# A three-stage kernel on one core: the first pair of token blocks by plain products, the sums and differences of w_in's blocks made later

## The chip, the cores and the metric

One core of a Trainium2 chip runs the whole program. The metric is device time in microseconds (us). Five engines work side by side, each through its own instructions in order: TensorE (PE in the profile), VectorE (DVE), ScalarE (ACT), GpSimd (POOL) and SyncE (SP), which here issues every DMA.

## What is computed

Attention within chunks of 64 tokens, then a two-matrix block with a squared Relu, then a gated block. The inputs q, k and v and the output are float32, the weights float64. The reference, cut to what matters:

```python
scores = scale * np.matmul(q_c, k_c.transpose(0, 1, 2, 4, 3))   # 8 batches, 8 heads, 9 chunks of 64, head size 64
attn = np.exp(scores - np.max(scores, axis=-1, keepdims=True))
attn = attn / (np.sum(attn, axis=-1, keepdims=True) + 1e-09)
x = np.matmul(attn, v_c)                                        # brought to [4608 tokens, 512]
...
h = np.maximum(x @ w_in, 0.0)                                   # w_in 512 x 2048
x = h * h @ w_out                                               # w_out 2048 x 512
...
gate = 1.0 / (1.0 + np.exp(-(x @ w_gate)))                      # 512 x 1536
return gate * (x @ w_val) @ w_out2                              # 1536 x 512
```

The kernel turns the weights from float64 words into float32 itself.

## The kernel before

**Products.** Each float32 operand is split into a high and a low part in the type fp32r (`split`: ScalarE copies the high part, VectorE subtracts it from the source to get the low part, L437). A product of two operands of K = 256 is six matmuls: two slices of K, and for each high x high, low x high and high x low. The helper `product` (L628) issues them.

**Seven products instead of eight.** A matrix product of 2 x 2 blocks would take eight block products. The class `Unit` does it with seven: P1 to P7, by Winograd's form of Strassen's scheme. For this the weights need four operands: "a" (the blocks a11 and a12 as they are), "s" and "t" (sums and differences of blocks, made by GpSimd with four operations of 256 columns, L446) and "d" (half of b). The tokens need B11, B21, B22 and four differences T1 to T4. The results are put together by additions on VectorE out of the PSUM banks.

**The stage x @ w_in.** The 4608 tokens go in 6 pairs of blocks of 384 (`BL1`). For each pair `s`, eight units `g` cover the 2048 columns of w_in: unit g computes column tiles g and g + 8 for both blocks. The pair's attention (six tiles of 128 tokens: `attention`, L738 to L837) runs one pair ahead: pair 1's attention is worked between the products of pair 0. While pair 0 runs, the weights are also made: `weight_group` loads two tiles of w_in (`to_float32`, two raw tiles `wraw` of 512 KB each), decodes them (ScalarE L479 and L483, VectorE L486, L488 and L495, GpSimd L502), and makes the operands `wia`, `wis`, `wit` and `wid`, which are kept in SBUF for all six pairs. `finish1` squares the Relu of each result and stores it to DRAM (`gd`).

**Who sets the order.** Nothing is issued directly. Each helper adds a job (engine, cost, reads, writes) to a list, and `Plan.run` puts all jobs in order with a list scheduler: each engine takes the ready job that is due first, with modelled costs; a job's due time follows from the TensorE jobs that need it, which have a fixed order ("main" for the products, "att" for the attention's own nominal times). A job that writes a new SBUF buffer also needs room for it in an arena of 412 x 512 bytes per partition; `look` says how long before its due time it may take that room. Every engine then runs its jobs in the planned order, and waits by semaphores.

The order of the products within the units, in which a unit's last three stages fall among the next one's:

```python
for make in [*todo, None]:
    u, more = make() if make is not None else (None, None)
    for who, p in ((u, "P1"), (last, "P7"), (u, "P2"), (u, "P5"), (last, "P3"), (last, "P4"), (u, "P6")):
        if who is not None:
            who.stage(p)
```

The stages behind this one (x @ w_out in `Long` units from L939 on, the gated block) use the same plan and are not touched, but the plan is made anew for the whole program.

Of the kernel before, what the change touches and what calls it, by code (L numbers as in the profile page):

```python
# [14 lines left out]
ALU = mybir.AluOpType  # L15
# [36 lines left out]
class Plan:  # L52
    def __init__(self, room):
        self.jobs, self.room = [], room
# [64 lines left out]
    def run(self):  # L119
# [51 lines left out]

        def take(j):
            got = []
            for b in j.allocs:
                if b.psum:
                    if not banks:
                        break
                    b.at = banks.pop(0)
                    got.append(b)
                elif b.size:  # L180
                    if not place(b):
                        break
                    got.append(b)
            else:
                return True
            for b in got:
                give(b)
                b.at = None
            return False
# [28 lines left out]
        while done < len(jobs):  # L218
            moved = True
            while moved:  # L220
                moved = False
                for e in engines:
# [23 lines left out]
                    while ready[e] and tries < 600:  # L246
# [3 lines left out]
                        need = sum(b.size for b in j.allocs)  # L250
                        ok = True
                        if need:
                            if due - t + shift > (j.look or (self.LOOK if e == "SP" else self.NEAR)):
                                ok = False
                            else:
                                held = 0
                                for d, m in wants:
                                    if d >= due or d > t - shift + self.HOLD:
                                        break
                                    if not jobs[m].started:  # L260
                                        held += sum(b.size for b in jobs[m].allocs)
# [66 lines left out]
def tile_attention_relu2_glu(  # L328
# [201 lines left out]
    def weight_group(src, f, half, name, keep, look=None, raws=None, by=None, have=None, slots=None, done=None):  # L530
# [12 lines left out]
        for kind, words in (("a", BLK), ("s", BLK), ("t", BLK), ("d", HB)):  # L543
# [5 lines left out]
            ops[kind] = Buf(8 * words, top=keep, name=f"{name[:-1]}{kind}", op=True)  # L549

# [18 lines left out]
        finished("a")  # L569
        s1, s2, s3, s4 = ((sums, i) for i in range(4))  # L570
# [43 lines left out]
    def product(ps, ops, xs, p, n, first, cost_of, at_=None):  # L614
        kind, half = A_OF[p]
        op, x = ops[kind], xs[B_OF[p]]
# [20 lines left out]
        return job("PE", 6 * cost_of, go, reads if first else [*reads, ps], [ps], stream="main", at=at_)  # L637
# [249 lines left out]

    def units(todo):
# [126 lines left out]
    with tc.manual_schedule():  # L1015
# [3 lines left out]
        span = 7 * G1 * 6 * per1  # L1019
        gb = {}  # L1020
# [26 lines left out]
        def attend(s):  # L1047
            for i in range(2 * TILES):
                def nominal(what, i=i):
# [3 lines left out]
                    return (s - 1) * span + slot * SLOT  # L1053
# [5 lines left out]
        todo = []  # L1059
        state = {}  # L1060

        def unit1(s, g):
            def make():
                if s == 0:
                    w1[g] = weight_group(w1i, g, G1, f"wi{g}", True, look=120.0)
                more = None
                if g == 0:
                    if s == 0:
                        attend(0)
# [10 lines left out]
        units([unit1(s, g) for s in range(pairs1) for g in range(G1)])  # L1080
# [196 lines left out]
```

## Time and profile before

| what | value |
|---|---|
| runs of the kernel | median 1678.0 us of 3 (1673.94 to 1683.32) |
| the profiled execution | 1678.82 us, its span 1677.0 us |
| mean granted TensorE clock | 0.988 |
| TensorE busy | 1623.2 us (97%) |
| VectorE busy | 1397.7 us (83%) |
| ScalarE busy | 981.9 us (59%) |
| GpSimd busy | 836.7 us (50%) |
| DMA | 333.35 MB, 63.8% of 16 engines' span |

The span runs from the first to the last instruction of the profiled execution; its time has 1.8 us around it. Busy times are sums over the instructions. The page also gives the busy share in 40 equal slices of the span, as one digit each (tenths), and the TensorE clock that was granted, as a share of full speed.

### The profile page before, as it was taken

How to read it: one execution, taken by the hardware profiler on the slowest of the kernel's cores; microseconds unless marked ns; L12 is line 12 of the kernel's file. 1: busy time of each engine (PE TensorE's matmuls, PEld its weight loads, DVE VectorE, ACT ScalarE, POOL GpSimd, SP SyncE). 2: the span in 40 equal slices, each digit the busy share in tenths (PEclk: the TensorE clock that was granted, in tenths of full speed). 3: DMA queues.
4: the chain of work that ended last, by engine and by line, in shares of the span. 5: the costliest groups of instructions: out<-in, count | busy, mean ns of one | idle time of the engine just before them, and what ended most of it. 6: DMA issues, size and time to landing. Idle time of an engine off the chain costs nothing. (4 is left out here: it accounts for less than half of the span.)

```text
span 1677.0 us, 30764 instructions
## 1 busy us (share of the span) xinstructions
PE 1623.2 (97%) x10452; PEld 1458.9 (87%) x10452; DVE 1397.7 (83%) x2024; ACT 981.9 (59%) x1974; POOL 836.7 (50%) x644
## 2 busy tenths in 40 slices
PE   6798999999999999999999999999999999999998
PEld 5688999999899999999997889878888889778887
DVE  7998687768689999999999997664776856999996
ACT  6675565666567655655666566544555544454553
POOL 2643020212165345353566887743655755877662
PEclk9899999999999999999999999999999999999999
DMA  9925556585697555755994754586265569665562
GB/s 242 219 78 145 161 149 179 141 233 150 201 307 258 164 170 198 255 179 164 322 330 141 255 195 147 196 324 230 111 232 201 206 250 340 170 171 145 169 173 49
DMA packets 390798, 333.35 MB, mean 199 GB/s; under 512 B 234736, under 2 KB 325616, under 8 KB 390640
## 3 DMA queue, kind: packets, MB, share of 16 engines
q1 hardware_dynamic: 390640, 331.38, 63.8%
q8 instruction: 82, 1.34, 0.3%
q14 instruction: 76, 0.62, 0.1%
HBM read 209.13 MB, written 122.16 MB: 198 GB/s over the span
## 5 line engine op out<-in xcount | busy, mean ns | idle before, releaser
L502 POOL TENSOR_TENSOR wf__2708<-wf__2708,wr__2646 128x512 int32<-128x512 int32 x16 | 21.1, 1320 | 216.9 <-DVE wf__2708 L495 163.5
L502 POOL TENSOR_TENSOR wf__7364<-wf__7364,wr__6450 128x512 int32<-128x512 int32 x18 | 25.1, 1397 | 86.1 <-DVE wf__7364 L495 54.7
L446 POOL TENSOR_TENSOR raw__537<-raw__696,raw__537 128x384 f32<-128x384 f32 x24 | 28.7, 1211 | 59.8 <-DVE B__706 L437 26.5
L502 POOL TENSOR_TENSOR wf__6816<-wf__6816,wr__6450 128x512 int32<-128x512 int32 x18 | 28.1, 1561 | 48.7 <-DVE wf__6816 L495 31.2
L483 ACT ACTIVATE wr__6450<-wr__6450 128x512 int32<-128x512 uint32 x36 | 23.9, 664 | 0.0
L437 DVE TENSOR_TENSOR wx__7302<-ws__7507,wx__7302 128x512 fp32r<-128x512 f32 x18 | 18.6, 1032 | 4.2 <-ACT wx__7302 L432 4.2
L437 DVE TENSOR_TENSOR wx__7676<-ws__7507,wx__7676 128x512 fp32r<-128x512 f32 x18 | 17.7, 986 | 4.5 <-ACT wx__7676 L432 4.3
L446 POOL TENSOR_TENSOR ws__7507<-wf__6816,wf__7364 128x256 f32<-128x256 f32 x18 | 17.2, 956 | 0.4
L446 POOL TENSOR_TENSOR ws__7507<-ws__7507,wf__6816 128x256 f32<-128x256 f32 x18 | 16.1, 897 | 1.3
L502 POOL TENSOR_TENSOR w__669<-w__669,wraw__374 128x512 int32<-128x512 int32 x1 | 1.4, 1378 | 30.4 <-ACT B__729 L432 30.4
L437 DVE TENSOR_TENSOR wx__7419<-wf__7364,wx__7419 128x256 fp32r<-128x256 f32 x18 | 16.4, 909 | 0.0
L488 DVE TENSOR_SCALAR wf__7364<-wf__7364 128x512 int32<-128x512 int32 x18 | 15.6, 867 | 0.6
L479 ACT ACTIVATE wf__6816<-wr__6450 128x512 f32<-128x512 f32 x18 | 12.0, 664 | 6.4 <-POOL ws__7507 L446 3.3
L446 POOL TENSOR_TENSOR raw__537<-raw__537 128x384 f32<-128x384 f32 x12 | 15.1, 1275 | 0.0
L486 DVE TENSOR_SCALAR wf__7364<-wf__7364 128x512 f32<-128x512 f32 x18 | 10.6, 590 | 5.3 <-ACT wf__7364 L479 5.3
L495 DVE SCALAR_TENSOR_TENSOR wf__7364<-wr__6450,wf__7364 128x512 int32<-128x512 int32 x18 | 14.7, 818 | 0.1
L479 ACT ACTIVATE wf__2708<-wr__2646 128x512 f32<-128x512 f32 x16 | 10.8, 672 | 6.6 <-DMA wf<-wf__2708 5.2
L446 POOL TENSOR_TENSOR raw__696<-raw__696 128x384 f32<-128x384 f32 x12 | 14.6, 1235 | 0.0
L495 DVE SCALAR_TENSOR_TENSOR wf__6816<-wr__6450,wf__6816 128x512 int32<-128x512 int32 x18 | 13.9, 774 | 0.2
L417 ACT ACTIVATE c__1728<-c__1728 128x384 f32<-128x384 f32 x20 | 10.4, 520 | 6.3 <-DVE c__1728 L446 6.2
L486 DVE TENSOR_SCALAR wf__6816<-wf__6816 128x512 f32<-128x512 f32 x18 | 9.0, 502 | 6.0 <-ACT wf__6816 L479 6.0
L837 ACT ACTIVATE raw__537<-bank 128x256 f32<-128x256 f32 x36 | 12.1, 381 | 2.0 <-DVE T__973 L437 1.3
(5624 smaller groups left out, 6528.8 us busy)
## 6 DMA issues: line engine op xcount, KB each, us to landing
ad<-wx__7302 SPq DMA_DIRECT2D x27, 512.0 KB, 4.8
ad<-wx__7676 SPq DMA_DIRECT2D x27, 512.0 KB, 4.5
wr__2646<-in_moe_w_out_dram SPq DMA_DIRECT2D x16, 512.0 KB, 4.8
wr__6450<-in_moe_w_gate_dram SPq DMA_DIRECT2D x12, 512.0 KB, 5.4
wr__6450<-in_moe_w_val_dram SPq DMA_DIRECT2D x12, 512.0 KB, 4.7
wr__6450<-in_moe_w_out_dram SPq DMA_DIRECT2D x12, 512.0 KB, 3.9
ad<-wx__7419 SPq DMA_DIRECT2D x18, 256.0 KB, 4.4
wf<-wf__2708 SPq DMA_DIRECT2D x16, 256.0 KB, 5.2
```

The source lines that it names most:

```text
L417: lambda: nc.scalar.activation(out=o(), in_=i(), func=func, **kw), ib, ob, soon=soon,
L437: lambda: nc.vector.tensor_tensor(out=lo(), in0=at(src, n, F32, off), in1=hi().bitcast(F32), op=ALU.subtract),
L446: eng, cost(eng, n), lambda: e.tensor_tensor(out=o(), in0=a(), in1=b(), op=op),
L479: nc.scalar.activation(out=at(w), in_=t[:, :, 1].bitcast(F32), func=ACTF.Abs)
L483: nc.scalar.activation(out=low, in_=low.bitcast(U32), func=ACTF.Copy, scale=2.0**-29)
L486: nc.vector.tensor_scalar_max(at(w), at(w), TINY)
L488: nc.vector.tensor_scalar(out=wi, in0=wi, scalar1=5, scalar2=2, op0=ALU.logical_shift_left, op1=ALU.logical_shift_right,)
L495: nc.vector.scalar_tensor_tensor(out=wi, in0=words()[:, :, 1], scalar=-0x40000000, in1=wi, op0=ALU.bitwise_and, op1=ALU.bitwise_or,)
L502: nc.gpsimd.tensor_tensor(out=wi, in0=wi, in1=words()[:, :, 0], op=ALU.add)
L837: nc.scalar.activation(out=o[:, :, a:a + CH], in_=i, func=ACTF.Copy)
```

## The change

For pair 0 the units g = 0 to 7 are no longer `Unit`s but plain ones: `plain_unit` makes the four results of a 2 x 2 block product by eight products, each result two products into one bank. It needs the weight operands "a" (first tile of w_in, both halves) and a new "l" (`wil`, the second tile, both halves; a buffer that is free again after pair 0), and the token operands B11, B21, B12 and B22; B12 uses the slots of T1. `finish0` takes a result from its bank: Relu on ScalarE, then a square, on VectorE for two of the four results (bank times Relu), on ScalarE for the other two. The units' own order is no longer interleaved in pair 0.

In `weight_group`, "s", "t" and "d" get a longer `look` (60 instead of 30) and come behind "l" in the list; their first use is in pair 1, which sets their due times. The buffers for s and t of all eight groups are given their places at the start of the plan (`plan.first`). The attention of pair 1 is listed after the weights of unit 1, with its nominal times stretched by 8/7.

```diff
 class Plan:
     def __init__(self, room):
-        self.jobs, self.room = [], room
+        self.jobs, self.room, self.first = [], room, []
...
+        for b in self.first:
+            place(b)
...
             ops[kind] = Buf(8 * words, top=keep, name=f"{name[:-1]}{kind}", op=True)
+            if keep and not have and kind in "st":
+                plan.first.append(ops[kind])
...
         finished("a")
+        if late:
+            ops["l"] = Buf(8 * BLK, name="wil", op=True)
+            split(ops["l"], b, BLK, look=look)
+            look = late
...
+    def plain_unit(ops, xs, n, per, finish):
+        u = Unit(ops, xs, n, per, finish, "")
+        for row, col in ((0, 0), (1, 0), (0, 1), (1, 1)):
+            ps = psum("C")
+            for half in range(2):
+                multiply(ps, ops["al"[row]], half, xs[f"B{half + 1}{col + 1}"], n, half == 0, per)
+            finish(u, row, col, ps)
...
+        span0 = 8 * G1 * 6 * per1
...
-                    return (s - 1) * span + slot * SLOT
+                    if s == 1:
+                        return slot * SLOT * 8 / 7
+                    return span0 + (s - 2) * span + slot * SLOT
...
+        def finish0(g):
+            def finish(u, row, col, ps):
+                n, f = BL1, g + row * G1
+                t = sbuf(n, "e")
+                copy(u.words(t), [t], u.words(ps), [ps], n, func=ACTF.Relu)
+                if row == col:
+                    binary("DVE", u.words(t), u.words(ps), u.words(t), ALU.mult, n, [t], [t, ps])
+                else:
+                    copy(u.words(t), [t], u.words(t), [t], n, func=ACTF.Square, soon=4.0)
...
+        attend(0)
+        first_xs = {}
+        for (r, c), x in blocks1(raw1).items():
+            name = f"B{r + 1}{c + 1}"
+            first_xs[name] = slots1["T1" if name == "B12" else name]
+            for op, (src, off) in zip(first_xs[name], x):
+                split(op, src, BL1, off=off)
+        for g in range(G1):
+            w1[g] = weight_group(w1i, g, G1, f"wi{g}", True, look=30.0, late=60.0)
+            if g == 1:
+                attend(1)
+            plain_unit(w1[g], first_xs, BL1, per1, finish0(g))
...
-                if s == 0:
-                    w1[g] = weight_group(w1i, g, G1, f"wi{g}", True, look=120.0)
...
-        units([unit1(s, g) for s in range(pairs1) for g in range(G1)])
+        units([unit1(s, g) for s in range(1, pairs1) for g in range(G1)])
```

`multiply` is `product` with the operands given to it. The plan places the same kinds of jobs in another order. Three places follow, in rows of each engine's order: line of the kernel (a line of the changed kernel is some 5 to 14 higher than its like before), operation, written and read tiles. The numbers in a tile's name are its place in memory.

TensorE, from the first product of pair 0 on, before (B and T are token operands, wia, wis and wit weight operands; a row is three matmuls, half a product):

```order
L628 MATMUL bank_78<-B_3072_29696__706,wia_186368__800 128x384 x3
L628 MATMUL bank_78<-B_3072_21504__729,wia_186368__800 128x384 x3
L628 MATMUL bank_74<-B_3072_18432__750,wia_186368__800 128x384 x3
L628 MATMUL bank_74<-B_3072_26624__761,wia_186368__800 128x384 x3
L628 MATMUL bank_75<-T_3072_195584__791,wis_182272__832 128x384 x3
L628 MATMUL bank_75<-T_3072_192512__793,wis_182272__832 128x384 x3
L628 MATMUL bank_78<-T_3072_175104__871,wis_182272__832 128x384 x3
L628 MATMUL bank_78<-T_3072_172032__877,wis_182272__832 128x384 x3
L628 MATMUL bank_73<-B_3072_29696__706,wia_165888__890 128x384 x3
L628 MATMUL bank_73<-B_3072_21504__729,wia_165888__890 128x384 x3
L628 MATMUL bank_78<-T_3072_162816__918,wit_178176__836 128x384 x3
L628 MATMUL bank_78<-T_3072_159744__921,wit_178176__836 128x384 x3
```

and in the change (768 is a transpose of k or q, 785 the scores of an attention tile):

```order
L641 MATMUL bank_74<-B_3072_44032__762,wia_129024__734 128x384 x3
L641 MATMUL bank_74<-B_3072_40960__767,wia_129024__734 128x384 x3
L785 MATMUL bank_75<-kT_22528__779,qT_38912__786 64x64 x16
L641 MATMUL bank_74<-B_3072_125952__769,wia_129024__734 128x384 x3
L641 MATMUL bank_74<-B_3072_122880__777,wia_129024__734 128x384 x3
L641 MATMUL bank_73<-B_3072_44032__762,wil_18432__751 128x384 x3
L641 MATMUL bank_73<-B_3072_40960__767,wil_18432__751 128x384 x3
L641 MATMUL bank_73<-B_3072_125952__769,wil_18432__751 128x384 x3
L641 MATMUL bank_73<-B_3072_122880__777,wil_18432__751 128x384 x3
L768 MATMUL bank_77<-ident,k_51200__747 128x128 x4
L641 MATMUL bank_76<-T_3072_48128__818,wia_129024__734 128x384 x3
L641 MATMUL bank_76<-T_3072_113664__827,wia_129024__734 128x384 x3
```

Before, the first unit needs wis and T1 after two products; now it needs wia, wil and B operands alone, with the attention's groups among them.

VectorE, before, in the first unit of pair 0 (790, 791 and 794 belong to the softmax, 486, 488 and 495 to a weight's decode, 437 is the low part of a split, 446 an addition out of a bank):

```order
L437 TENSOR_TENSOR wia_186368__800<-w_38912__763,wia_186368__800 128x512
L790 TENSOR_REDUCE mx_2048__852<-bank_72 128x8
L437 TENSOR_TENSOR wis_182272__832<-sums_34816__752,wis_182272__832 128x512
L791 TENSOR_TENSOR a_108544__875<-bank_72,mx_2048__852 128x512
L437 TENSOR_TENSOR T_3072_175104__871<-raw_6144_204800__537,T_3072_175104__871 128x384
L437 TENSOR_TENSOR T_3072_172032__877<-raw_6144_204800__537,T_3072_172032__877 128x384
L486 TENSOR_SCALAR w_55296__798<-w_55296__798 128x512
L488 TENSOR_SCALAR w_55296__798<-w_55296__798 128x512
L437 TENSOR_TENSOR wia_165888__890<-w_100352__783,wia_165888__890 128x512
L794 TENSOR_REDUCE mx_2048__852<-a_108544__875 128x8
L437 TENSOR_TENSOR wit_178176__836<-sums_34816__752,wit_178176__836 128x512
L446 TENSOR_TENSOR e_110592__885<-e_110592__885,bank_74 128x384
```

and in the change, around the first split of an s operand (807 to 812 belong to the softmax, 491 to 500 to a decode, 442 is a split, 451 the finishing multiply):

```order
L442 TENSOR_TENSOR wia_83968__1454<-w_28672__1144,wia_83968__1454 128x512
L807 TENSOR_REDUCE mx_24064__1299<-a_19968__1479 128x8
L810 TENSOR_SCALAR mx_24064__1299<-mx_24064__1299 128x8
L811 RECIPROCAL mx_24064__1299<-mx_24064__1299 128x8
L812 TENSOR_TENSOR a_19968__1479<-a_19968__1479,mx_24064__1299 128x512
L442 TENSOR_TENSOR wil_96256__1477<-w_24576__741,wil_96256__1477 128x512
L491 TENSOR_SCALAR w_26624__799<-w_26624__799 128x512
L493 TENSOR_SCALAR w_26624__799<-w_26624__799 128x512
L500 SCALAR_TENSOR_TENSOR w_26624__799<-wraw_55296__444,w_26624__799 128x512
L451 TENSOR_TENSOR e_0__1553<-bank_75,e_0__1553 128x384
L442 TENSOR_TENSOR wis_206848__1107<-sums_88064__996,wis_206848__1107 128x512
L442 TENSOR_TENSOR wia_92160__1569<-w_22016__1288,wia_92160__1569 128x512
```

Before, wis and wit of a unit stand within ten rows of its wia; now wis of unit 0 (wis_206848) stands behind wil of unit 5 (wil_96256), in the second half of pair 0.

SP, before, where the loads of w_in are issued (wraw are the raw tiles of w_in, k, q and v the attention's inputs):

```order
L410 DMA wraw_51200__406<-in_moe_w_in_dram 128x4x256
L410 DMA k_512__408<-in_k_dram 128x8x64
L410 DMA q_55296__415<-in_q_dram 128x8x64
L410 DMA wraw_59392__419<-in_moe_w_in_dram 128x4x256
L410 DMA wraw_63488__429<-in_moe_w_in_dram 128x4x256
L410 DMA wraw_67584__431<-in_moe_w_in_dram 128x4x256
L410 DMA wraw_71680__452<-in_moe_w_in_dram 128x4x256
L410 DMA wraw_75776__455<-in_moe_w_in_dram 128x4x256
L410 DMA wraw_79872__464<-in_moe_w_in_dram 128x4x256
L410 DMA wraw_6144__466<-in_moe_w_in_dram 128x4x256
L410 DMA wraw_83968__475<-in_moe_w_in_dram 128x4x256
L410 DMA wraw_88064__493<-in_moe_w_in_dram 128x4x256
```

and in the change, at the loads for units 4 to 6 (gd are stores of pair 0's results):

```order
L415 DMA wraw_63488__860<-in_moe_w_in_dram 128x4x256
L415 DMA v_69120__872<-in_v_dram 128x8x64
L415 DMA gd_88<-e_67584__870 128x384
L415 DMA gd_80<-e_4608__846 128x384
L415 DMA gd_80<-e_73216__913 128x384
L415 DMA wraw_79872__934<-in_moe_w_in_dram 128x4x256
L415 DMA k_76800__944<-in_k_dram 128x8x64
L415 DMA q_19968__949<-in_q_dram 128x8x64
L415 DMA wraw_6144__625<-in_moe_w_in_dram 128x4x256
L415 DMA gd_88<-e_18432__946 128x384
L415 DMA v_85504__985<-in_v_dram 128x8x64
L415 DMA gd_81<-e_83968__983 128x384
```

Before, all sixteen loads go out before the first store; now the last six stand among the loads of the next attention and the stores of pair 0's first results.

## Rows read from the trace of the kernel before

**Rows 1.** The page, the span in 40 equal slices, busy tenths of TensorE:

```profile
PE   6798999999999999999999999999999999999998
```

**Rows 2.** Stretches: us from:to, length, busy us (instructions) by engine, granted clock, DMA:

```profile
29.87:135.30 105.43, 80.42 (x783) 71.68 (x784) 103.30 (x155) 73.85 (x155) 62.85 (x56) 0.86 0.64 165
43.19:155.03 111.84, 94.31 (x816) 86.17 (x815) 104.72 (x164) 73.97 (x157) 60.89 (x54) 0.90 0.59 147
155.03:215.00 59.97, 58.32 (x605) 54.03 (x604) 43.47 (x84) 35.19 (x77) 2.67 (x3) 1.00 0.57 154
160.00:1677.00 1517.00, 1497.49 (x9121) 1347.17 (x9119) 1257.09 (x1803) 874.54 (x1751) 763.23 (x574) 1.00 0.63 202
```

The engines stand in the order PE, PEld (weight loads), DVE, ACT, POOL.

**Rows 3.** TensorE's waits from 0 to 160 us: total us, times, longest:

```profile
PE bank L628 <- DVE e__1147 L446: 3.0, 1, 3.0
PE bank L628 <- DVE wia__800 L437: 3.0, 1, 3.0
...
PE bank L628 <- DVE T__918 L437: 2.4, 1, 2.4
```

**Rows 4.** TensorE in order of time: start, us, line, tiles, shape, count:

```profile
43.19 0.69 PE L628 MATMUL bank<-B__706,wia__800 128*128 128x384 f32 x1
...
47.66 1.16 PE L628 MATMUL bank<-B__729,wia__800 128*128 128x384 f32 x3
...
99.71 0.69 PE L822 MATMUL bank<-aT__1212,v__838 64*64 64x64 f32 x32
100.34 0.79 PE L628 MATMUL bank<-T__871,wis__1267 128*128 128x384 f32 x3
100.97 0.68 PE L628 MATMUL bank<-T__877,wis__1267 128*128 128x384 f32 x3
101.49 0.68 PE L628 MATMUL bank<-B__706,wia__1369 128*128 128x384 f32 x3
...
102.63 1.15 PE L772 MATMUL bank<-kT__1373,qT__1377 64*64 64x64 f32 x32
103.70 0.79 PE L628 MATMUL bank<-T__918,wit__1337 128*128 128x384 f32 x3
...
105.90 0.60 PE L806 MATMUL bank<-ident,a__1396 128*128 128x128 f32 x4
106.33 0.60 PE L755 MATMUL bank<-ident,k__935 128*128 128x128 f32 x4
...
154.51 0.69 PE L628 MATMUL bank<-T__973,wid__1812 128*128 128x384 f32 x3
...
156.88 0.44 PE L628 MATMUL bank<-T__871,wis__832 128*128 128x384 f32 x1 [0.46 <-DVE T__871 L437]
...
158.17 0.45 PE L628 MATMUL bank<-T__877,wis__832 128*128 128x384 f32 x1 [0.50 <-DVE T__877 L437]
```

**Rows 5.** VectorE in order of time, within one unit of pair 0:

```profile
105.73 1.78 DVE L437 TENSOR_TENSOR wis__1402<-sums__1349,wis__1402 128x512 fp32r<-128x512 f32 x1
107.44 0.68 DVE L790 TENSOR_REDUCE mx__1371<-bank 128x8 f32<-128x512 f32 x1
108.04 0.54 DVE L446 TENSOR_TENSOR b__1398<-b__1398,bank 128x384 f32<-128x384 f32 x1
108.50 0.59 DVE L437 TENSOR_TENSOR wid__1387<-w__847,wid__1387 128x256 fp32r<-128x256 f32 x1
...
110.08 0.41 DVE L486 TENSOR_SCALAR w__1470<-w__1470 128x512 f32<-128x512 f32 x1
110.52 0.43 DVE L488 TENSOR_SCALAR w__1470<-w__1470 128x512 int32<-128x512 int32 x1
110.86 0.68 DVE L437 TENSOR_TENSOR wia__1517<-w__1244,wia__1517 128x512 fp32r<-128x512 f32 x1
```

**Rows 6.** A load of w_in (KB, us from issue to landing); SP's waits, 0 to 160 us:

```profile
wraw__499<-in_moe_w_in_dram SPq DMA_DIRECT2D x1, 512.0 KB, 9.7
...
SPq L410 <- ACT raw__537 L837: 8.2, 1, 8.2
```

More of the change, by code (lines that the diff above doesn't have):

```diff
@@ L174, in take @@
             for b in j.allocs:
+                if b.at is not None:
+                    continue
                 if b.psum:
@@ L249, in run @@
                         tries += 1
-                        need = sum(b.size for b in j.allocs)
+                        need = sum(b.size for b in j.allocs if b.at is None)
                         ok = True
@@ L260, in run @@
                                     if not jobs[m].started:
-                                        held += sum(b.size for b in jobs[m].allocs)
+                                        held += sum(b.size for b in jobs[m].allocs if b.at is None)
                                 if due - t + shift > self.FAR:
@@ L528, in float32_in_dram, with weight_group @@
         return load
-    def weight_group(src, f, half, name, keep, look=None, raws=None, by=None, have=None, slots=None, done=None):
+    def weight_group(src, f, half, name, keep, look=None, raws=None, by=None, have=None, slots=None, done=None, late=None):
         by = by or columns
@@ L615, in product, with multiply @@
         kind, half = A_OF[p]
-        op, x = ops[kind], xs[B_OF[p]]
+        multiply(ps, ops[kind], half, xs[B_OF[p]], n, first, cost_of)
+    def multiply(ps, op, half, x, n, first, cost_of):
         size = op.size // 8
@@ L635, in go @@
                     )
-        return job("PE", 6 * cost_of, go, reads if first else [*reads, ps], [ps], stream="main", at=at_)
+        return job("PE", 6 * cost_of, go, reads if first else [*reads, ps], [ps], stream="main")
     def token_ops(blocks, n, slots=None):
@@ L1057, in blocks1 @@
             return {(r, c): [(raws[c], (2 * r + kk) * BL1) for kk in range(2)] for r in range(2) for c in range(2)}
-        todo = []
+        def finish0(g):
[7 more added lines that the diff above has]
+                    copy(u.words(t), [t], u.words(t), [t], n, func=ACTF.Square, soon=4.0)
+                a = col * BL1
+                d = gb[f, col] = Buf(name="g")
+                dma(lambda: gd[f][:, a:a + n], lambda: at(t), [t], [d], size=P * n * 4, soon=6.0)
+            return finish
+        attend(0)
[10 more added lines that the diff above has]
+            plain_unit(w1[g], first_xs, BL1, per1, finish0(g))
         state = {}
@@ L1063, in make @@
             def make():
-                if s == 0:
-                    w1[g] = weight_group(w1i, g, G1, f"wi{g}", True, look=120.0)
                 more = None
                 if g == 0:
-                    if s == 0:
-                        attend(0)
                     state["xs"], rest = token_ops(blocks1(raw1), BL1, slots1)
```

## The prediction

> **What bounds the kernel now.** I read the page first for the whole span, then the stretches of the first 320 us, then the waits of TensorE there, then single instructions. The page shows TensorE busy to 9 tenths or more in nearly every one of its 40 slices of 42 us, except in the first two (6 and 7), the fourth (8) and the last (8) [rows 1]. So there are two regimes: a start in which TensorE is short of operands, and some 1500 us in which it is the bound. In the stretches [rows 2] TensorE idles 1517.0 - 1497.5 = 19.5 us after 160 us, little for so long a stretch; from 155 to 215 us it idles 1.65 us in 60. The loss lies ahead of that.
>
> VectorE is why. From 29.87 us (first decode of w_in) to 135.30 us (last weight operand of pair 0) it is busy 103.3 of 105.4 us [rows 2], and TensorE's waits in the start are mostly for VectorE: for e (a bank that an addition still reads), wia (a weight operand) and T (a token operand) [rows 3].
>
> How much does TensorE lose? Pair 0's products start at 43.19 us, and the last half of its last one starts at 154.51 us [rows 4]; until 155.03 us that is 111.84 us. A product is two rows of three matmuls at 0.52 us (100.97 to 101.49), so 1.04 us; the attention in between has groups of 0.43 (four transposes), 0.63 (mixing with v) and 1.07 us (scores) [rows 4]. In that stretch stand 59 products (56 of pair 0, 3 of pair 1), 13 + 6 transposed groups, 6 scores, 6 mixes: 61.4 + 8.2 + 6.4 + 3.8 = 79.8 us. So 32.0 us are lost, in waits and in time at the lower clock: the mean granted clock there is 0.90, and at 47.66 us three matmuls show 1.16 us, at 100.97 us 0.68 [rows 2, 4].
>
> **The change, TensorE.** In pair 0 a unit goes from 7 to 8 products: 8 units x 1.04 us = 8.3 us more, all on the path, for good. The rest of TensorE's program has the same products. To compare, take "pair 0 is done". Before, by 155.03 us TensorE had also done 3 products of pair 1, and three transposed groups and one score group that the new order holds until later: 3.1 + 1.3 + 1.1 = 5.5 us. So the equal point before is 149.5 us. After, pair 0 has 64 products, 8 + 6 transposed groups, 6 scores and 6 mixes behind its first product: 66.6 + 6.0 + 6.4 + 3.8 = 82.8 us. The start stays near 43.2 us: the four raw tiles, and k and q, are still loaded one after another, and the order puts two more transposed groups ahead. The gain is 149.5 - 43.2 - 82.8 - L = 23.5 - L, where L is what TensorE will still lose.
>
> **The change, VectorE.** Alone, from start to next start [rows 5]: 0.60 us for 512 wide, 0.46 for 384, 0.44 and 0.34 for the two decode steps (0.40 in the mean); 0.35 for 256 wide, 0.22 for the small ones, from the same pattern. Before, 29.87 to 135.30 us holds 62 of 512, 44 of 384, 32 decode steps, 12 small, 6 of 256: 37.2 + 20.2 + 12.8 + 2.6 + 2.1 = 74.9 us. It took 105.4, so 30.5 us are stretching. A row shows it: wis takes 1.78 us while GpSimd works, an equal wia 0.68 [rows 5]. GpSimd was busy 62.85 us in 56 instructions, 1.12 us each [rows 2]; so each busy microsecond of GpSimd costs VectorE 30.5 / 62.85 = 0.49 us.
>
> After, from the first decode to the last row of pair 0, the order has 63 of 512 (the splits of l added; most of s and t still there, since wis and wit of units 0 to 3 are made before pair 0 ends), 23 of 384 (8 token splits instead of 14; two finishing multiplies a unit instead of five additions and squares), 32 decode steps, 12 small, 3 of 256, one transpose of 0.7: 37.8 + 10.6 + 12.8 + 2.6 + 1.1 + 0.7 = 65.6 us. GpSimd has 16 decodes and 24 sums ahead of that point, and none of the ten token differences: 40 x 1.12 = 44.8 us, which stretch VectorE by 22 us. So VectorE could be through at 29.9 + 65.6 + 22 = 117.5 us, where TensorE by its own sum is done at 43.2 + 82.8 = 126 us. **The bound moves from VectorE to TensorE**, but narrowly. By the same sums wia of unit 2 is there at about 53, unit 4 at 83, unit 6 at 99 us and wil of unit 7 at about 115; TensorE, at 10.35 us a unit and 3 us late from its start, wants them at 67, 88, 108 and 121. The margin is 5 to 14 us, and VectorE spends some of it: six times, it must wait in order for a score product, with the weight splits queued behind that wait, and a finishing multiply now waits in its queue for a product and for ScalarE's Relu. I take 1 to 6 us of margin as left.
>
> **L.** At the lower clock three matmuls took 1.16 instead of 0.68 us [rows 4], so about half of such a time is lost; for some 6 us of it at the start, 3 us. Further waits lie between 2.3 us (the rate of 155 to 215 us, 1.65 in 60 [rows 2], over 83 us) and 14 us (half of the 32.0, from the same stretch while VectorE was the bound). Nearest is the first, as the operands are early by the sum, but the margin is thin: 5 us. L = 8.
>
> **What goes to pair 1.** VectorE still has 9 splits of s and t and 5 of d behind the last row of pair 0 (9 x 0.60 + 5 x 0.35 = 7.2 us), and GpSimd 8 sums (9.0 us, 4.4 of stretch). VectorE is busy 43.5 of 60 us in that stage [rows 2], so it has 16 us spare per 60 us: covered, unless it all stands before the first T operands. Those must wait anyway for the last product that reads their slots; the same hand-over before shows waits of 0.46 and 0.50 us for T, at 156 and 158 us [rows 4]. I add 1.5 us for it, between 0 and all 11.6.
>
> **SP's queue.** Before, all 16 loads of w_in went out in a row; the longest took 9.7 us to land [rows 6]. Now the loads for units 5 to 7 stand between stores of pair 0's results, and a store waits for its unit. For about three units, 31 us, each load runs ahead of its product; landing and preparing it need 9.7 us and about 5 us of decode and split. Cost: nothing, as that lead covers it.
>
> Sum: 23.5 - 8 - 1.5 = 14.0 us gained, of the profiled execution's 1678.8 us, which lies 0.8 us above the median of the runs. From the median: **1664.0 us**. Where the tables of the later stages come out differently by the new plan, I allow 3 us either way, about a sixth of the 19.5 us idle there.
>
> **A rule that speaks against it.** VectorE's operations that read PSUM kept 0.54 us (108.04) right between stretched ones [rows 5], so it is the ones with SBUF operands that GpSimd slows. The Trainium skill (SBUF — State Buffer, "Who interferes with whom") says that the two hold a shared port as an exclusive lock, by which the later one blocks fully. The trace agrees on which operations are hit; by the lock taken at its worst, a whole microsecond lost per busy one, the 22 us of stretch would be 44.8.
>
> **The rivals.**
>
> *VectorE stays the bound.* If its remaining mix suffers a full microsecond per busy one of GpSimd instead of 0.49, it ends at 29.9 + 65.6 + 44.8 = 140.3 us, wil of unit 7 some 2 us earlier, and 6 products (6.2 us) follow: 144.5 against 149.5. With the hand-over 3.5 us stay gained, and gaps at the lower clock take most of that: 1677. For it: the share of two-operand splits in VectorE's work rises. Against: 0.49 was measured on much the same mix. Chance 0.08.
>
> *The deferred work bunches at pair 1.* If the 11.6 us all fall before the first T operands, the gain is 23.5 - 8 - 11.6 = 4: 1674. For it: five d and nine s and t splits stand among the token splits there in the order. Against: TensorE needs them one unit at a time. Chance 0.10. Waits in pair 0 near their upper end give the same (23.5 - 17 - 1.5 = 5, 1673): 0.03.
>
> *Slower: the loads turn into a ring.* A load behind a store, the store behind a product, the product behind an earlier load. SP has waited 8.2 us for a single buffer [rows 6]. The lead of 31 us covers 15 us of landing and preparing and two such waits; from a third in a row on, each of units 5 to 7 comes 8 us late, 24 us, and after each gap TensorE runs at the lower clock for a while, some 4 us lost in all: L = 8 + 28, and 23.5 - 36 - 1.5 = -14: 1692. For it: two slots of raw tiles are loaded again in the middle of pair 0, one of them twice. Against: a lead of three units. Chance 0.06.
>
> *The change does not defer.* The order shows wis of unit 0 behind wil of unit 5, so this is out; only part of the deferral is small, as s and t of four units are still made in pair 0. That is in the sum.
>
> *More than forecast.* No waits beyond the first clock ramp and no hand-over: 23.5 - 3 = 20.5, 1657.5, or less with luck later. Chance 0.07.
>
> **How the numbers follow.** Forecast (1657.5 to 1669.6) 0.66, more 0.07, the no-change rivals 0.08 + 0.10 + 0.03, slower 0.06. A difference of 0.5%, 8.4 us, is about what a measurement here can tell from none: faster means under 1669.6. Faster 0.66 + 0.07 = 0.73; same 0.21; slower 0.06. The range goes from 1655 (1657.5 less most of the 3 us) to 1678: above it lie the ring and part of the first rival, below it little.
>
> **What would show it.** Right: first product of pair 0 at 42 to 45 us; VectorE no longer filled from 60 to 120 us; GpSimd without token differences until pair 0 is over; the last half product of pair 0 at 128 to 138 us instead of 154.5; TensorE's waits for wia and wil few and under 1 us; after that the same spacing as before. Wrong: wil splits ending just as their products start, or T waits of several microseconds at pair 1; a gap on TensorE with an SP wait for a store behind it; or a gain in pair 0 that is lost again after 215 us.

## The result and the profile after

The changed kernel takes 1662.68 us, the median of 4 runs (1661.88 to 1663.56), beside 1678.37 us of 4 runs of the kernel before (1673.94 to 1683.32): ratio 0.9906, 95% interval 0.9878 to 0.9934. The forecast was 1664.0 with a range of 1655 to 1678 and 0.73 for faster by over 0.5%. The total came out as forecast, but not by the forecast's terms: the first pair of token blocks (pair 0) gained half as much again as it was to gain, and a third of that was given back behind it.

The page of the kernel after, busy tenths in 40 slices and the granted clock, beside [rows 1]:

```profile
PE   7999999999999999999999999999999999999998
DVE  7998677767789999999999797754777757999995
POOL 1552103030454443543577677733675646867672
PEclk8999999999999999999999999999999999999999
```

The second slice (42 to 83 us) went from 7 to 9 and the fourth from 8 to 9: the start has lost its holes. TensorE is busy 1621.5 us of the span of 1661.8 us (98%), where it was 1623.2 of 1677.0, although pair 0 has 8 products more: less of the work was done at the lower clock (the granted clock in pair 0 is 0.98 below, 0.90 in [rows 2]).

Stretches of the kernel after; the columns are those of [rows 2]. The first is pair 0 on TensorE, the second goes from the first decode of w_in to VectorE's last row of pair 0, the third is the rest:

```profile
39.50:126.36 86.86, 86.86 (x827) 82.92 (x826) 81.03 (x127) 70.38 (x146) 45.94 (x43) 0.98 0.70 191
29.17:121.78 92.61, 88.55 (x882) 83.35 (x883) 86.14 (x136) 76.70 (x161) 47.32 (x44) 0.94 0.74 194
155.00:1661.80 1506.80, 1479.76 (x8915) 1333.77 (x8913) 1240.75 (x1778) 864.82 (x1732) 764.61 (x578) 0.99 0.64 202
```

In pair 0 TensorE is busy 86.86 of 86.86 us; before it was 94.31 of 111.84. VectorE, filled before to 103.30 of 105.43 us, is busy 86.14 of 92.61; of the 6.5 us that it is idle, 1.6 are waits for score products and about 3 are waits for ScalarE. Behind 155 us it is the other way round: TensorE idles 1506.80 - 1479.76 = 27.0 us, where it idled 19.5 [rows 2].

TensorE in order of time (columns as in [rows 4]): the first product, the last weights of pair 0, its last half product, and the hand-over to pair 1:

```profile
39.50 1.31 PE L641 MATMUL bank<-B__762,wia__734 128*128 128x384 f32 x3
...
120.12 0.68 PE L641 MATMUL bank<-B__762,wil__1817 128*128 128x384 f32 x3
...
125.84 0.68 PE L641 MATMUL bank<-B__842,wil__1817 128*128 128x384 f32 x3
126.36 0.68 PE L641 MATMUL bank<-B__762,wia__734 128*128 128x384 f32 x3
...
134.10 0.45 PE L641 MATMUL bank<-T__2020,wis__1107 128*128 128x384 f32 x1 [0.63 <-DVE T__2020 L442]
...
135.39 0.45 PE L641 MATMUL bank<-T__2022,wis__1107 128*128 128x384 f32 x1 [0.49 <-DVE T__2022 L442]
```

Pair 0 ends at 126.36 us with none of pair 1's products done; the equal point before was 149.5 us. So 23.1 us are gained there. The spans differ by 15.2 us (1677.0 - 1661.8), so 7.9 us were given back behind pair 0. The hand-over is little of that: its two T waits above take 1.1 us, but the same two waits took 0.96 us before [rows 4]. About 7.7 us were lost later, which fits the idle time (27.0 against 19.5). Where, the stretches show. Of the kernel before:

```profile
300.00:480.00 180.00, 175.28 (x1643) 165.77 (x1643) 138.12 (x251) 113.62 (x250) 44.22 (x38) 0.98 0.68 192
480.00:800.00 320.00, 318.85 (x1834) 317.23 (x1833) 304.61 (x483) 202.21 (x424) 143.44 (x124) 1.00 0.63 207
```

and of the kernel after:

```profile
300.00:480.00 180.00, 175.12 (x1582) 166.01 (x1573) 135.38 (x245) 116.30 (x257) 49.14 (x44) 0.99 0.73 211
480.00:800.00 320.00, 314.85 (x1793) 311.19 (x1792) 309.89 (x483) 197.42 (x408) 149.49 (x122) 0.99 0.64 211
```

The idle time is alike up to 480 us, and 1.15 against 5.15 us from 480 to 800 us, where the stage with w_out begins; the rest is spread over the stretches behind. The edit does not touch that stage.

VectorE in order of time in the kernel after, up to its last row of pair 0:

```profile
101.37 0.69 DVE L803 TENSOR_REDUCE mx__1299<-bank 128x8 f32<-128x512 f32 x1 [1.00 <-PE bank L785]
...
116.90 1.23 DVE L442 TENSOR_TENSOR wit__1516<-sums__1259,wit__1516 128x512 fp32r<-128x512 f32 x1
118.05 1.22 DVE L442 TENSOR_TENSOR wil__1817<-w__1701,wil__1817 128x512 fp32r<-128x512 f32 x1
...
121.23 0.55 DVE L451 TENSOR_TENSOR e__1857<-bank,e__1857 128x384 f32<-128x384 f32 x1
```

The last wil is there at 118.05 + 1.22 = 119.27 us, 0.85 us before its first product at 120.12. The bound has moved, with little to spare.

### The profile page after: what moved, and what is told of

Read it like the earlier page. It is cut to its first block, busy times and chain, and to the rows that moved or that the text cites. A ratio compares the mean times of both kernels' runs of the same rounds, so it can differ in the third digit from the quotient of the medians.

```text
span 1661.8 us, 30842 instructions
## 1 busy us (share of the span) xinstructions
PE 1621.5 (98%) x10500; PEld 1463.8 (88%) x10500; DVE 1375.4 (83%) x2002; ACT 979.9 (59%) x1968; POOL 822.3 (49%) x636
## 5 line engine op out<-in xcount | busy, mean ns | idle before, releaser
L451 POOL TENSOR_TENSOR raw__514<-raw__674,raw__514 128x384 f32<-128x384 f32 x20 | 23.5, 1195 | 69.2 <-DVE B__762 L442 48.8
L451 POOL TENSOR_TENSOR ws__7370<-ws__7370,wf__6751 128x256 f32<-128x256 f32 x18 | 15.7, 870 | 1.3
L493 DVE TENSOR_SCALAR wf__7084<-wf__7084 128x512 int32<-128x512 int32 x18 | 14.2, 790 | 0.6
L484 ACT ACTIVATE wf__6751<-wr__6460 128x512 f32<-128x512 f32 x18 | 12.0, 665 | 4.7 <-POOL ws__7370 L451 4.7
L500 DVE SCALAR_TENSOR_TENSOR wf__7084<-wr__6460,wf__7084 128x512 int32<-128x512 int32 x18 | 14.4, 801 | 0.2
L442 DVE TENSOR_TENSOR B__762<-raw__514,B__762 128x384 fp32r<-128x384 f32 x6 | 3.4, 566 | 13.0 <-ACT B__762 L437 13.0
L484 ACT ACTIVATE wf__7084<-wr__6460 128x512 f32<-128x512 f32 x18 | 11.9, 659 | 2.8 <-DMA wr__6460<-in_moe_w_gate_dram 2.8
L484 ACT ACTIVATE wf__3381<-wr__3279 128x512 f32<-128x512 f32 x16 | 10.6, 665 | 4.3 <-DMA wf<-wf__3381 4.2
L451 DVE TENSOR_TENSOR b__12368<-b__12368,bank 128x512 f32<-128x512 f32 x5 | 3.4, 687 | 11.3 <-PE bank L641 11.3
L493 DVE TENSOR_SCALAR wf__6751<-wf__6751 128x512 int32<-128x512 int32 x18 | 12.3, 682 | 0.6
```

The costliest lines, as they stand in the source:

```text
L442: lambda: nc.vector.tensor_tensor(out=lo(), in0=at(src, n, F32, off), in1=hi().bitcast(F32), op=ALU.subtract),
L451: eng, cost(eng, n), lambda: e.tensor_tensor(out=o(), in0=a(), in1=b(), op=op),
L484: nc.scalar.activation(out=at(w), in_=t[:, :, 1].bitcast(F32), func=ACTF.Abs)
L493: nc.vector.tensor_scalar(out=wi, in0=wi, scalar1=5, scalar2=2, op0=ALU.logical_shift_left, op1=ALU.logical_shift_right,)
L500: nc.vector.scalar_tensor_tensor(out=wi, in0=words()[:, :, 1], scalar=-0x40000000, in1=wi, op0=ALU.bitwise_and, op1=ALU.bitwise_or,)
```

## The experiments

**The theory** after this result: in the start VectorE, slowed by GpSimd, was the bound; the change takes the sums and additions off it until TensorE is the bound, and that is worth 23 us. **A first rival**: the start gains because products come earlier in the order, and VectorE's load matters little. **For what was given back** there are two more: the later loss belongs to the change (late s, t and d), or it is the plan, since the scheduler writes the order of everything behind pair 0 anew.

**1. The plain products without the deferral.** Sums and splits of s, t and d are due at once, in the kernel after:

```diff
+        soon = 1.0 if late else None
...
-        split(ops["s"], sums, BLK, look=look)
+        split(ops["s"], sums, BLK, look=look, soon=soon)
```

and so for the sums, t and d.

> The changed kernel, with the s, t and d operands of each group of w_in due at once again, as the a and l operands are; pair 0 stays with plain products. Theory (VectorE sets the pace only when its queue is full; the deferral takes 9 splits of s and t, 5 of d and 8 sums out of pair 0, 11.6 us of VectorE): pair 0's last half product, at 125.8 us in the changed kernel, comes 3 to 9 us later, and the time is 1665 to 1672. Rival 1 (the plain products give the whole gain, the deferral none): 125 to 127 us and 1661 to 1665. Rival 2 (the deferral gives the whole gain): 145 us or later, 1676 or more.

Measured: 1666.87 us (1662.37 to 1669.43, 5 runs), ratio to the kernel before 0.9928 (0.9906 to 0.9951). Pair 0 in this run, on TensorE and by stretch:

```profile
134.44 0.68 PE L642 MATMUL bank<-B__837,wil__1911 128*128 128x384 f32 x3
```

```profile
39.78:134.96 95.18, 90.35 (x839) 85.04 (x837) 91.84 (x139) 75.52 (x157) 49.54 (x44) 0.97 0.71 187
```

The last half product comes 8.6 us later than in the kernel after (134.44 against 125.84), with 4.8 us of idle time in the stretch where there was none; VectorE is busy 91.84 of 95.18 us again. The largest waits are for a (2.4 and 1.2 us), the softmax whose steps stand in VectorE's queue between the splits. By its last half product this run has also done 12 transposes more of the attention than the kernel after by its own (108 against 96, three groups of 0.43 us). So the deferral does part of the work, about 7 of the 23 us of pair 0. The whole kernel, however, is only 4.2 us slower than after, within the 1665 to 1672 expected: it makes up some 3 us behind pair 0, with 23.2 us of idle time behind 155 us instead of 27.0.

**2. The kernel before without its sums.** s and t are not made, the products of pair 0 and later read a in their place:

```diff
+        if keep and not have:
+            ops["s"] = ops["t"] = ops["a"]
+            split(ops["d"], b, HB, off=HB, look=look)
+            return ops
```

> The kernel before, seven products, but s and t of w_in are not made: the products that want them read the a operand instead (the four sums of each group and the two splits behind them are left out). Theory (in the kernel before, VectorE's and GpSimd's work on these operands is what holds pair 0 up): VectorE loses 16 x 0.60 us and the stretch by 32 sums, about 24 us; the products of pair 0 start at 39 to 44 us, the equal point of 149.5 us comes at 117 to 125 us, and the time is 1648 to 1658. Rival (the loads of w_in, or the token differences, hold it up anyway): the equal point after 140 us, and 1668 or more.

Measured: 1657.86 us (one run). The last half product of pair 0 there, which is row 154.51 of [rows 4]:

```profile
133.82 0.68 PE L632 MATMUL bank<-T__928,wid__1927 128*128 128x384 f32 x3
```

It stands 20.7 us earlier than before, with TensorE's products unchanged, and the time is 19.7 us less than the 1677.55 us of the kernel before on that chip. VectorE's and GpSimd's work on s and t, not the order of the products, set the length of pair 0. The first rival falls. The run takes away the work and the products' wait for its results together, so it does not part these two. The expectation held for the time (1648 to 1658) and was too hopeful for pair 0: its equal point, reckoned as before, comes at about 128 us and not at 117 to 125, though its first product comes at 36.01 us, ahead of the 39 to 44 expected.

**3. Two more VectorE operations a unit, in the kernel after.** They are 512 wide and their result is not used:

```diff
+            for _ in range(2):
+                x = sbuf(BLK, "extra")
+                binary("DVE", lambda x=x: at(x), lambda: at(a), lambda: at(b), ALU.subtract, BLK, [x], [a, b], soon=2.0)
```

> The changed kernel with two more VectorE operations of 128x512 with two SBUF inputs in each of the eight groups of pair 0 (16 x 0.60 us and their stretch, 10 to 14 us; their results are used by nobody). Theory (TensorE is the bound in pair 0 now, and VectorE has s, t and d to put off further): pair 0's last half product at 126 to 129 us, against 125.8, and 1660 to 1668. Rival (VectorE is still the bound): 135 us or later, and 1671 or more.

Measured: 1673.81 us (one run). Pair 0's last half product, and a wait behind it:

```profile
128.82 0.68 PE L644 MATMUL bank<-B__844,wil__751 128*128 128x384 f32 x3
...
136.76 1.15 PE L788 MATMUL bank<-kT__2007,qT__1857 64*64 64x64 f32 x32 [2.46 <-ACT kT__2007 L422]
```

Pair 0 ends 3.0 us later, as expected: 16 operations, at least 9.6 us by the 0.60 us of one, are absorbed to two thirds. Room for them came from putting off more: by the end of pair 0 only 3 of the 16 splits of s and t are done and none of d, where the kernel after has 9 and 3. The total was expected at 1660 to 1668 and missed that by 6 us: 8 us are lost behind pair 0 (2.46 at once, at the hand-over, where ScalarE's copy of kT stands behind four others in its queue, and 3 us more of idle time behind 155 us than after). Whether the work put off costs this, or the new plan, is not shown.

**4. Without the fixed places for s and t.** In the kernel after:

```diff
-        for b in self.first:
-            place(b)
```

> The changed kernel without the places given to the s and t buffers at the start of the plan; they take their room when they are written. Theory (the fixed places serve the room in memory and cost pair 0 nothing): pair 0's last half product at 125 to 128 us, and 1658 to 1668, as the later stages are planned anew. Rival (64 KB more room in pair 0 brings the loads of w_in earlier and with them pair 0's end): 123 us or earlier. Rival (the room for s and t then comes late): the hand-over to pair 1 waits 5 us or more.

Measured: 1772.38 us (one run). The page, and one of TensorE's waits:

```profile
PE   7999700699999999999999999999999999999998
```

```profile
PE bank L638 <- ACT wit__3097 L434: 105.1, 1, 105.1
```

The last half product of pair 0 starts at 125.94 us, as after. But between 160 and 330 us TensorE stands still for 105.1 us in one piece, for t of the last unit. ScalarE's copy for this t stands in its queue behind twelve decodes of w_out, each of which waits 7.2 to 8.7 us for the store of the one before. The expected 1658 to 1668 failed; nearest is the rival by which the room comes late, but it priced 5 us or more, at the hand-over. The change's least visible line is what makes the deferral safe. That the plan puts t behind those decodes for want of room in SBUF is argued from what the line does; the trace shows the wait and the order.

**5. The same kernels in other plans.** In both kernels the attention of all pairs behind pair 1 (the expectations name pairs 2 and 3, the edit reaches pairs 2 to 5) is due somewhat later or earlier, and nothing else is changed. In the kernel after (shift 0.7; the others -0.7, 0.3 and 1.5):

```diff
-                    return span0 + (s - 2) * span + slot * SLOT
+                    return span0 + (s - 2) * span + slot * SLOT + 0.7
```

In the kernel before the shift is added to (s - 1) * span + slot * SLOT, for s over 1.

> The kernel after, with the due times of the attention of pairs 2 and 3 shifted by 0.7 us, and nothing else: the same work, the planner writes the order of everything behind pair 0 anew. Theory (the 7 to 8 us that went missing between the gain of pair 0, 23.1 us, and the gain of the whole, 15.2 us, are the luck of one plan): pair 0 ends within 1.5 us of 125.8, TensorE's idle time behind 155 us is not 27 but anywhere from 18 to 33 us, and the time moves by as much, 1653 to 1669. Rival (the loss belongs to the change: later s, t and d, fewer free slots, weights that come late): idle time stays at 25 to 29 us and the time within 2 us of 1662.7.

> As the run before, with a shift of 1.5 us. Theory: 1653 to 1669, idle behind 155 us 18 to 33 us, and different from the other shift by 3 us or more. Rival: 1661 to 1665 and 25 to 29 us of idle time, as after.

> The kernel before, with the same shift of 0.7 us for pairs 2 and 3. Theory: the 19.5 us of idle time behind 160 us are one plan's as well; 1671 to 1686, idle 14 to 28 us. If the plan before had been the lucky one, both shifts of it give 1680 to 1686 and both of after 1655 to 1662. Rival: within 2 us of 1677.6.

> The kernel before, with a shift of 1.5 us. Theory: 1671 to 1686, idle behind 160 us 14 to 28 us, and different from the other shift by 3 us or more. Rival: within 2 us of 1677.6.

> The kernel after, the attention of pairs 2 and 3 due 0.7 us earlier instead of later. The shifts to later cost 26 and 30 us behind pair 0 (12 us of it one wait for w_out's first operand). Theory A (luck of the plan: each plan is a draw, and the one of after was a good one): 1662 to 1692, nothing gained on average against 1662.7. Theory B (it was the direction: later attention is worse, earlier is not): within 4 us of 1662.7. Theory C (the change makes the later stages frailer than before): after's loss by this shift is more than 10 us above that of before by the same shift. In all: pair 0 ends at 125 to 127 us.

> The kernel after, shift of 0.3 us to later. A: 1662 to 1692, and not between the times of the shifts 0 and 0.7 in any order; B: 1663 to 1689, between them; C: as for the run before. Pair 0 ends at 125 to 127 us.

> The kernel before, the attention of pairs 2 and 3 due 0.7 us earlier. A: 1675 to 1692; B: 1674 to 1681; C: less loss than the kernel after has by this shift, by more than 10 us.

> The kernel before, shift of 0.3 us to later. A: 1675 to 1692; B: between 1677.6 and 1686.4; C: less loss than the kernel after has by this shift, by more than 10 us.

Measured, 4 runs each (9 of the kernel before with 0.3), medians in us, beside 1676.8 and 1677.1 of the unshifted kernel before on the same chips; "last" is the start of the last half product of pair 0, "rest" the span less that, "idle" TensorE's idle time behind 160 us (before) and 155 us (after):

| shift | before: time | last | rest | idle | after: time | last | rest | idle | difference of the times |
|---|---|---|---|---|---|---|---|---|---|
| -0.7 | 1689.27 | 155.12 | 1532.4 | 28.6 | 1659.72 | 125.46 | 1531.8 | 25.5 | -29.6 |
| 0 | 1678.37 | 154.51 | 1522.5 | 19.5 | 1662.68 | 125.84 | 1536.0 | 27.0 | -15.7 |
| 0.3 | 1684.03 | 155.09 | 1527.1 | 26.9 | 1667.95 | 126.38 | 1541.5 | 31.6 | -16.1 |
| 0.7 | 1686.36 | 154.63 | 1529.7 | 30.8 | 1689.01 | 126.38 | 1560.7 | 47.2 | +2.7 |
| 1.5 | 1687.75 | 151.08 | 1534.4 | 29.0 | 1692.31 | 126.14 | 1565.2 | 45.9 | +4.6 |

Three things follow.

The gain of pair 0 is firm: in five plans the last half product of the changed kernel starts between 125.46 and 126.38 us, that of the kernel before between 151.08 and 155.12.

The rest is not. It moves by 12 us over the plans of the kernel before and by 33 us over those of the kernel after, by shifts of 0.3 to 1.5 us. So 7.7 us lost behind pair 0 need no cause in the edit: the plan of the kernel before, with 19.5 us idle, is the best of its five. That all of it is such luck is not shown, and the pairs lean against it. In every plan 59 products are done when "last" is, before, and 64 after, so that the kernel before is ahead by 3 products of pair 1 and some attention, 5.5 us of work (5.1 with 0.7 and 3.5 with 1.5, where it has done less attention). The rest is longer after by -0.6, 13.5, 14.4, 31.0 and 30.8 us; less that work, one pair gains 6 us behind pair 0 and four lose 8 to 27. Five pairs do not part a loss by the change from the luck of the plans.

The expectations erred too: the kernel after with 0.7 and 1.5 is 20 us and more outside 1653 to 1669; the kernel before is 0.4 and 1.8 us above 1686, with 30.8 and 29.0 us idle where 14 to 28 were expected, and the two differ by 1.4 us and not by 3; with -0.7 the kernel after is below theory A's 1662 to 1692. The shift does not act like a draw on the kernel after, whose time rises with it in all five rows, as theory B said; on the kernel before it does not, since -0.7 costs 11 us there. Theory C holds for the two large shifts (26 and 30 us against 8 and 9) and fails for 0.3 (5.3 against 5.7) and for -0.7, where the kernel after loses nothing.

Where the plan with 0.7 loses, its trace shows. TensorE there:

```profile
525.54 1.20 PE L961 MATMUL bank<-x__6358,woa__6078 128*128 128x384 f32 x6
539.45 0.69 PE L961 MATMUL bank<-x__6482,woa__6101 128*128 128x384 f32 x1 [12.70 <-ACT woa__6101 L437]
540.67 1.97 PE L961 MATMUL bank<-x__6482,woa__6101 128*128 128x384 f32 x5 [0.53 <-DVE woa__6101 L442]
```

the stretch:

```profile
520.00:540.00 20.00, 7.30 (x40) 6.71 (x39) 19.53 (x26) 3.84 (x9) 13.56 (x12) 0.72 0.30 101
```

and VectorE in it:

```profile
526.93 1.21 DVE L442 TENSOR_TENSOR wod__6456<-w__5597,wod__6456 128x256 fp32r<-128x256 f32 x1
528.07 1.34 DVE L442 TENSOR_TENSOR x__6498<-g__6103,x__6498 128x384 fp32r<-128x384 f32 x1
529.33 1.07 DVE L451 TENSOR_TENSOR g__6160<-g__6383,g__6160 128x384 f32<-128x384 f32 x1
...
537.65 0.41 DVE L442 TENSOR_TENSOR wod__6473<-w__5711,wod__6473 128x256 fp32r<-128x256 f32 x1
...
540.19 0.42 DVE L442 TENSOR_TENSOR woa__6101<-w__5583,woa__6101 128x256 fp32r<-128x256 f32 x1
```

ScalarE in the same stretch:

```profile
532.30 0.52 ACT L437 ACTIVATE x__6507<-g__6115 128x384 fp32r<-128x384 f32 x1 [7.27 <-DVE wod__6465 L442]
538.57 0.52 ACT L437 ACTIVATE x__6522<-g__6130 128x384 fp32r<-128x384 f32 x1 [5.75 <-DVE wod__6488 L442]
539.00 0.40 ACT L437 ACTIVATE woa__6101<-w__5583 128x256 fp32r<-128x256 f32 x1
```

It is much like the start of pair 0, at the start of w_out: VectorE is busy 19.53 of 20 us, token differences and wod splits stand in its queue ahead of the one woa split that TensorE needs, GpSimd works beside it for 13.56 us, and a 256-wide split that takes 0.41 us takes 1.21. The long wait itself is for ScalarE's half of that split: it stands behind two token copies that wait 7.27 and 5.75 us for VectorE's wod splits. The wait of 12.7 us is about half of the 25 us that this plan loses on the plan of the kernel after; with the shift of 1.5 the same place costs 11.9 us; in the eight other plans of the two kernels no wait of TensorE from 500 to 570 us is over 3.8 us. Why a shift of attention brings those splits into that order was not traced further.

The plan with -0.7 of the kernel after is the lowest measured, 1659.72 us (1658.1 to 1661.4), ratio 0.9892 (0.9870 to 0.9914). That is 3 us below the kernel after, but the two intervals overlap.

## Why the prediction was right, and which of its terms were not

| term | predicted | measured |
|---|---|---|
| first product of pair 0 | 43.2 us | 39.50 us |
| TensorE's work in pair 0, and low clock | 82.8 us and 3 us | 86.86 us, so 4.1 over the sum, at the lower clock and in spacing |
| waits in pair 0 | 5 us | none |
| pair 0 done, gain on 149.5 us | 134 us, 15.5 us | 126.36 us, 23.1 us |
| hand-over to pair 1 | 1.5 us | 1.1 us, 0.2 more than before |
| later stages | 0, within 3 us | 7.7 us lost |
| sum | 14.0 us | 15.2 us of the spans |

**The mechanism** stood as put: the bound of pair 0 was VectorE and is TensorE now. Experiment 2 shows the first half by itself, the stretch of 86.86 us without idle time the second.

**VectorE's sum** was nearly exact. It was forecast to be busy 65.6 + 22 = 87.6 us up to the last row of pair 0, and was for 86.14 us, in 136 instructions where 134 were counted. GpSimd was busy 47.32 us there (44.8 forecast); (86.14 - 65.6) / 47.32 = 0.43 us of stretch for each of its busy microseconds, against 0.49 (which counts 2.1 us of VectorE's idle time as stretch; (103.3 - 74.9) / 62.85 is 0.45). The end at 121.78 instead of 117.5 us is waiting in order, 6.5 us in all, which the prediction named (score products, ScalarE's Relu) but did not add.

The prediction's worst case, a whole microsecond for each busy one of GpSimd, would be 65.6 + 47.3 = 112.9 us in a stretch of 92.61, and did not come. Single rows are blocked in full all the same. In the kernel before:

```profile
44.59 1.66 POOL L502 TENSOR_TENSOR w__774<-w__774,wraw__386 128x512 int32<-128x512 int32 x1 [0.63 <-DVE w__774 L495]
```

```profile
45.04 1.76 DVE L437 TENSOR_TENSOR wia__800<-w__763,wia__800 128x512 fp32r<-128x512 f32 x1
```

GpSimd's row ends at 46.25 us and VectorE's at 46.80, 0.55 us behind, which is the 0.68 us that such a row takes alone less 0.13. So it goes with 32 of the 33 rows with two SBUF operands, 256 to 512 wide, that began while a GpSimd row ran from 29.87 to 135.30 us, and with 19 of 20 from 29.17 to 121.78 us in the kernel after. The Trainium skill (SBUF — State Buffer, "Who interferes with whom") says that whoever issues first gets the shared pair of ports for the whole instruction and the other fully blocks; the rows agree. The sum stays under a whole microsecond because a row is held only for what is left of GpSimd's, and because rows that read PSUM, 0.55 us at 121.23, are not held.

**L, the first mis-sized term.** The prediction put 3 us of low clock and 5 us of waits. The waits did not come, although the margin was as thin as feared (0.85 us at the last wil): operands that arrived just in time cost nothing here. The lower bound of the waits, 2.3 us, was still too high.

**The start, the second.** "The start stays near 43.2 us" rested on the loads, which did stay. What moved was VectorE's queue. In the kernel before four token splits, three of them stretched to between 1.08 and 1.64 us by GpSimd's first decode, sums and differences, stood ahead of the decode and the split of wia__800, for which TensorE waited 2.97 us in its first product. One of those token splits (beside the decode), and that wait, in the kernel before:

```profile
31.86 1.64 DVE L437 TENSOR_TENSOR B__729<-raw__537,B__729 128x384 fp32r<-128x384 f32 x1
```

```profile
46.85 1.01 PE L628 MATMUL bank<-B__706,wia__800 128*128 128x384 f32 x2 [2.97 <-DVE wia__800 L437]
```

In the kernel after VectorE's queue reads:

```profile
33.81 1.67 DVE L442 TENSOR_TENSOR wia__734<-w__647,wia__734 128x512 fp32r<-128x512 f32 x1 [0.31 <-ACT wia__734 L437]
...
36.20 0.69 DVE L442 TENSOR_TENSOR wil__751<-w__684,wil__751 128x512 fp32r<-128x512 f32 x1
...
39.21 0.55 DVE L442 TENSOR_TENSOR B__762<-raw__514,B__762 128x384 fp32r<-128x384 f32 x1
39.68 0.54 DVE L442 TENSOR_TENSOR B__767<-raw__514,B__767 128x384 fp32r<-128x384 f32 x1
```

Both weight operands are ready, and the token splits run at full speed (0.54 and 0.55 us), since GpSimd, with only decodes to do, stands idle from 39.01 to 41.90 us. The prediction applied its 0.49 to pair 0 as a whole and not to these first 10 us; they came out 3.7 us shorter. This is read from the two traces; no run changed the start alone. In experiment 2, without the sums, the first product starts earlier still, at 36.01 us.

**The later stages, the term that failed.** "Where the tables of the later stages come out differently by the new plan, I allow 3 us either way", a sixth of the idle time there. The plans of experiment 5 move it by 11 us in the kernel before and by 22 in the kernel after. The allowance was taken from how much was idle in one plan, and one plan says nothing of the spread. It is by this that 23.1 us became 15.2. The errors, 7.6 us too little in pair 0, 7.7 us too little lost later and 1.3 us too much for the hand-over, nearly cancel: that the total lies within 2 us of the forecast is luck, while the mechanism of pair 0 is not.

**The rivals.** VectorE as the bound, the loads as a ring and the bunching at pair 1 are out: no wait of pair 0, no gap for a load, 1.1 us at the hand-over. "More than forecast" came true in pair 0 (it priced 20.5 us) and was taken back. Its own list had the sign to look for, "a gain in pair 0 that is lost again after 215 us": it happened to a third of the gain, and in the plans with 0.7 and 1.5 to more than all of it. Two of its signs of being right were missed, both towards more gain: the first product (39.50 us, not 42 to 45) and the last half product (125.84 us, not 128 to 138). A third came only in part: from 60 to 120 us VectorE is busy 54.95 us, where it was 58.32.

## What to carry to other kernels

Where a stage is short of operands because a helper engine is full, a little more work on the main engine (here 8.3 us) can buy much of that stage, if the helper's work can wait until it has time; cost the helper's sum with its stretch, also in the first microseconds. Reserve the room for what is made later: without it one wait of 105.1 us came. And where a scheduler writes the order, an edit at the start redraws everything behind it: look at the stage that was changed for the edit's worth, run the kernels before and after in several plans, and only then believe a difference of ten microseconds.

## What had not been expected

That a due time moved by 0.7 us, in a stage that the edit does not touch, costs 26 us: more than the edit gains in pair 0. Over the five pairs of plans the mean difference is -10.8 us with a standard deviation of 14 us, so five plans do not settle its sign, while the gain of pair 0, 21 to 24 us at equal work, stands in every one of them. And that the same queue, VectorE's splits stretched beside GpSimd, makes TensorE wait in two places far apart, at 45 us in the kernel before and at 530 us in a plan of the kernel after.
